# Gated MLP in a decode backward pass: w2 in blocks of 128 rows, and its second half mixed with head 0

## The chip, the core and the metric

The kernel runs on one core of a Trainium2 chip. The metric is device time in microseconds for one launch, taken as the median of repeated runs. Engine names are those of the profile: PE is TensorE's matmul, PEld its weight load, DVE is VectorE, ACT is ScalarE, POOL is GpSimd, SP is SyncE. A letter q after an engine's name means its queue of DMA issues or its sequencer.

## The reference

The kernel computes a forward pass and its vector-Jacobian product for one token. Everything is bf16.

```python
xn  = layernorm(x)                                   # x: 1 x 640
A   = attention(xn @ wq, k_cache, v_cache) @ wo      # 32 heads, 8192 keys, head size 128
B   = (silu(xn @ w1) * (xn @ w3)) @ w2               # gated MLP, 640 -> 1728 -> 640
out = x + A + B
# returned: out, and the gradients for x, k_cache, v_cache, wq, wo, w1, w3, w2
```

The K and V caches (67 MB each) are read once, and gradients of the same size are written. The MLP's three weights have 2.21 MB each; each is read, and a gradient of its size is written.

With the incoming gradient g, the MLP's backward pass needs dh = w2 g, then dgate and dup (1728 values each), and from these dw1 = xn times dgate, dw3 = xn times dup, dw2 = h times g, and a part of the gradient of xn that sums over w1 and w3.

## The kernel before

**Loads and stores.** All loads of weights and caches are issued by SP, in program order, and nearly all stores by POOL, in program order. An issue waits until the tile it fills is free, and everything behind it in the same queue waits too. DVE, SP, POOL and ACT run in the order in which the program was written (`ORDERED`, L58); only PE's order is left to a scheduler.

SP's order at the start is: x, w1 (L142), w3 (L144), w2 in three tiles (L149), wq and wo of the first group of heads, K of head 0, V of heads 0 and 1. `kpool` has three buffers (L68), and w1, w3 and K of head 0 take them. K of head 1 (`load_k(1)`, L544) therefore goes into the buffer of w1 once the store of w1's gradient has landed, and K of head 2 (L545) into that of w3 once its gradient's store has landed: both gradients are computed in place.

**The MLP** is a generator, `mlp_steps` (L440). Its first half runs ahead of `prep_steps(0)` (query and output gradient of the first four heads), its second half after it:

- First half. `gu_ps` (L444 to L449): gate and up as columns, 16 groups of 108 rows of the hidden size; per group five matmuls with a 128 x 108 weight tile of w1 or w3, each streaming one column. Then dh: for each of the three tiles of w2 (6, 5 and 5 groups, on 108 partitions) DVE multiplies by g (L459), PE sums over runs of 64 (L462), DVE finishes the sum (L455). Then a chain of small operations on DVE (L471 to L484) and the diagonal tile `diag` (L486).
- Second half. Eight matmuls spread dgate and dup over all partitions (L496), ACT and DVE copy them to `bc_sb` (L500, L502). Then w2 gives its part of the output (80 matmuls, L509), ACT writes w2's gradient over w2 (16 operations, L511) and POOL stores it in three DMAs (L512). Last, for w1 and then for w3: DVE multiplies the weight by `bc_sb` (three operations, L518), PE sums them into `dx_ps` (54 matmuls, L521), DVE writes the gradient over the weight (L524) and POOL stores it (L528). The tiles `T` that DVE fills for PE have two buffers (`tpool`, L72), which L518 shares with the heads' products.

Since POOL's queue is in order, the store of w1's gradient stands behind all three stores of w2's.

**The heads.** The loop over h (L547) interleaves head h with the start of head h+1. It starts at h = -1, where only the first half of head 0's work is done: `product` S twice (L333 on DVE, L335 on PE), `row_max`, `product` DP twice around `exps`. From h = 0 on, each head has four products for the next head and four `outer` stores of 1 MB each (L342 on DVE, L346 on ACT, L348 on POOL). V of head h+2 and K of head h+3 are loaded as the buffers come free.

Of the kernel before, what the change touches and what calls it, by code (L numbers as in the profile page):

```python
# [16 lines left out]
P = 128  # L17
# [4 lines left out]
def kernel(  # L22
# [38 lines left out]
    R2 = 16  # L61
    FR = F // R2
    ACT_J = 8
    assert H % GW == 0 and GW % GH == 0 and F % R2 == 0 and FR <= P and P % GH == 0
# [29 lines left out]
    w2_v = B_w2.rearrange("(r q) c -> q r c", r=R2)  # L94
    dw2_v = out_8.rearrange("(r q) c -> q r c", r=R2)

    with tc.manual_schedule(engines=ORDERED):
# [43 lines left out]
        w1t = kpool.tile([P, NC, F], BF16, name="w1t", tag="K")  # L141
        nc.sync.dma_start(w1t[:], w1_v)  # L142
        w3t = kpool.tile([P, NC, F], BF16, name="w3t", tag="K")
        nc.sync.dma_start(w3t[:], w3_v)  # L144
        w2_parts = []
        r0 = 0
        for rows in (6, 5, 5):
            w2c = opool.tile([P, rows, D], BF16, name="w2c", tag="o")
            nc.sync.dma_start(w2c[0:FR], w2_v[:, r0:r0 + rows, :])  # L149
            w2_parts.append((r0, rows, w2c))  # L150
            r0 += rows
        assert r0 == R2
# [287 lines left out]
        def mlp_steps():  # L440
# [3 lines left out]
            gu_ps = ps_w.tile([P, 2, R2], F32, name="gu_ps", tag="w")  # L444
            for wi, wt in enumerate((w1t, w3t)):
                for r in range(R2):
                    for ci in range(NC):
                        nc.tensor.matmul(gu_ps[0:FR, wi, r:r + 1], lhsT=wt[:, ci, r * FR:(r + 1) * FR],
                                         rhs=xn_col_bf[:, ci:ci + 1], start=(ci == 0), stop=(ci == NC - 1))  # L449
            dhc = small.tile([P, R2], F32, name="dhc", bufs=1)  # L450
            sums = []

            def dh_reduce():
                r0, rows, dh_ps = sums.pop(0)
                nc.vector.tensor_reduce(dhc[0:FR, r0:r0 + rows], dh_ps[0:FR], AX.X, ALU.add)  # L455

            for k, (r0, rows, w2c) in enumerate(w2_parts):
                T2 = tpool.tile([P, rows, D], BF16, name="T2", tag="T")
                nc.vector.tensor_tensor(T2[0:FR], w2c[0:FR], g_bc_bf[0:FR].unsqueeze(1).to_broadcast([FR, rows, D]), ALU.mult)  # L459
                dh_ps = ps_w.tile([P, rows, DRUN], F32, name="dh_ps", tag="w")  # L460
                for i in range(D // DRUN):
                    nc.tensor.matmul(dh_ps[0:FR], lhsT=ident_bf[0:FR, 0:FR], rhs=T2[0:FR, :, DRUN * i:DRUN * (i + 1)],  # L462
                                     start=(i == 0), stop=(i == D // DRUN - 1))
                sums.append((r0, rows, dh_ps))
                if k:
                    dh_reduce()
            dh_reduce()
            sm_f = small.tile([P, 9, R2], F32, name="sm_f", bufs=1)
            gate, up, th, sig, silu, hcol, t1, dgate, dup = (sm_f[0:FR, i, :] for i in range(9))
            dgu = sm_f[0:FR, 7:9, :]  # L470
            nc.vector.tensor_copy(sm_f[0:FR, 0:2, :], gu_ps[0:FR])  # L471
            nc.scalar.activation(th, gate, ACTF.Tanh, scale=0.5)
            dh = dhc[0:FR]
            nc.vector.tensor_scalar(sig, th, 0.5, 0.5, ALU.mult, ALU.add)
            nc.vector.tensor_tensor(silu, gate, sig, ALU.mult)
            nc.vector.tensor_tensor(dup, dh, silu, ALU.mult)
# [4 lines left out]
            nc.vector.tensor_tensor(dgate, dh, up, ALU.mult)  # L481
            nc.vector.tensor_tensor(dgate, dgate, t1, ALU.mult)
            dgu2 = small.tile([P, 2, R2, 2], BF16, name="dgu2", bufs=1)
            nc.vector.tensor_copy(dgu2[0:FR], dgu.unsqueeze(3).to_broadcast([FR, 2, R2, 2]))  # L484
            diag = opool.tile([P, 2, R2, FR // 2, 2], BF16, name="diag", tag="o")
            nc.vector.tensor_tensor(diag[0:FR],  # L486
                                    ident_bf[0:FR, 0:FR].rearrange("p (a b) -> p a b", b=2).unsqueeze(1).unsqueeze(1)
                                    .to_broadcast([FR, 2, R2, FR // 2, 2]),
                                    dgu2[0:FR].unsqueeze(3).to_broadcast([FR, 2, R2, FR // 2, 2]), ALU.mult)
            bc_sb = opool.tile([P, 2, F], BF16, name="bc_sb", tag="o")  # L490
            yield
            RC = 4
            for wi in range(2):
                for r0 in range(0, R2, RC):
                    bc_ps = ps_w.tile([P, RC, FR], F32, name="bc_ps", tag="w")
                    nc.tensor.matmul(bc_ps[:], lhsT=ones_bf[0:FR, :],  # L496
                                     rhs=diag[0:FR, wi, r0:r0 + RC].rearrange("p r a b -> p r (a b)"), start=True, stop=True)
                    part = bc_sb[:, wi, r0 * FR:(r0 + RC) * FR].rearrange("p (r q) -> p r q", r=RC)
                    if wi == 0 and r0 % (2 * RC) == 0:
                        nc.vector.tensor_copy(part, bc_ps[:])  # L500
                    else:
                        nc.scalar.copy(part, bc_ps[:])  # L502
            nc.vector.tensor_tensor(hcol, silu, up, ALU.mult)
            hcol_bf = small.tile([P, R2], BF16, name="hcol_bf", bufs=1)
            nc.vector.tensor_copy(hcol_bf[0:FR], hcol)
# [36 lines left out]
        for _ in mlp:  # L542
            pass
# [3 lines left out]
        for h in range(-1, H):  # L547
            n = new_head(h + 1) if h + 1 < H else None
            c = hs.pop(h) if h >= 0 else None
            if h >= 0:  # L550
                g, hh = divmod(h, GH)
# [5 lines left out]
            if c:  # L557
                probs(c)
                outer(c, c.do, c.P2, c.Pf, dvc, h, 0)
                if prev:  # L560
                    keep_dq(prev)
# [99 lines left out]
```

## Time and profile before

| | us |
|---|---|
| median of 3 runs (lowest to highest) | 761.67 (760.68 to 762.18) |
| the profiled execution: its own time | 761.41 |
| the profiled execution: span of instructions | 759.4 |
| moved in the span | 303.72 MB, mean 400 GB/s |
| DVE busy | 632.5 (83%) |
| PE busy | 557.3 (73%) |
| ACT busy | 474.4 (62%) |

The profile shows for each engine its busy time, for each of 40 slices of 19 us the busy share in tenths, the granted clock of PE, and what the 16 DMA engines moved. A view by stretches gives the same for any stretch of time: busy time of each engine (with the number of instructions), the granted clock, the share of time that the DMA engines were busy, and GB/s. The timeline lists instructions in order: start, duration, engine, line, operation, what is written from what, and in brackets how long the engine was idle before and what ended that. A view of waits sums idle time by what ended it; the chain is the work that ended last, followed back from the last instruction.

### The profile page before, as it was taken

Reading aid. Unit: us, or ns where it says so; the run is one execution under the profiler, and the core shown is the slowest. Engines: PE = TensorE matmul, PEld = TensorE weight load, DVE = VectorE, ACT = ScalarE, POOL = GpSimd, SP = SyncE. Lnnn points to the kernel's source line nnn. Section 1 sums busy time; section 2 is a strip of 40 time slices with the busy share of each in tenths; the row PEclk is TensorE's granted clock in tenths of the full one; section 3 lists DMA queues with packets and bytes.
Section 4 is the critical chain, followed back from the end, with each engine's and each line's share of the span. In section 5 each row is a group of like instructions: output and inputs, shape, how many; then the busy total and the mean of one; then the engine's idle time right before and its main releaser. Section 6 shows DMA issues by size and latency. Waiting matters only on the chain.

```text
span 759.4 us, 15976 instructions
## 1 busy us (share of the span) xinstructions
PE 557.3 (73%) x6528; PEld 337.3 (44%) x6543; DVE 632.5 (83%) x706; ACT 474.4 (62%) x1421; POOL 87.5 (12%) x166
## 2 busy tenths in 40 slices
PE   6865888878688773877777765788786778777860
PEld 5652445544454442544443433444353445444440
DVE  2577999999799894998788994999887998899970
ACT  2180567777666763787655963778564957677672
POOL 0010011111001120110100120111000111011120
PEclk9987778787886687787896987777795888877665
DMA  8969799999999999999999999999999999999795
GB/s 298 335 258 366 301 428 425 423 422 418 430 427 428 423 416 426 426 423 417 429 428 426 426 377 430 424 427 419 430 425 427 428 418 427 428 427 424 325 363 201
DMA packets 37355, 303.72 MB, mean 400 GB/s; under 512 B 4120, under 2 KB 5874, under 8 KB 12194
## 3 DMA queue, kind: packets, MB, share of 16 engines
q1 hardware_dynamic: 15190, 151.35, 48.5%
q0 software_dynamic: 22080, 151.35, 48.4%
q8 instruction: 51, 0.84, 0.4%
q14 instruction: 22, 0.18, 0.1%
q10 hardware_dynamic: 12, 0.00, 0.0%
HBM read 151.34 MB, written 151.34 MB: 399 GB/s over the span
## 4 chain that ended last, share of the span: by engine, by line
DMA 55%; DVE 31%; PE 6%; issue 4%; ACT 2%; SPq 1%; POOL 0%; POOLq 0%; DVEq 0%; ACTq 0%
DMA out_dram<-ot 39%; DVE T L333 14%; DVE ot L342 11%; DMA out_dram<-wo_g 9%; DMA wo_g<-in_A_wo_dram 4%; DMA w2c<-in_B_w_dram 3%; PE psS L335 2%; ACT ot L346 1%; DVE S_sb L352 1%; DVE DP_sb L386 1%; PE psDP L335 1%; PE dx_ps L521 1%; DVE w3t L524 1%; DVE T L518 1%; SPq L149 0%
## 5 line engine op out<-in xcount | busy, mean ns | idle before, releaser
L335 PE MATMUL psDP<-T,ident_bf 128*128 128x512 bf16 x512 | 187.2, 529 | 65.3 <-DVE T L333 65.3
L335 PEld LDWEIGHTS <-ident_bf 128*128 128x128 bf16 x1024 | 120.2, 120 | 221.8 <-issue 167.0
L346 ACT ACTIVATE ot<-qs_g,Uf 128x128 bf16<-128x128 bf16 x512 | 156.4, 389 | 68.6 <-DMA out_dram<-ot 55.9
L346 ACT ACTIVATE ot<-do_g,Pf 128x128 bf16<-128x128 bf16 x512 | 156.3, 389 | 13.4 <-DMA out_dram<-ot 12.5
L333 DVE TENSOR_TENSOR T<-Kt,qs_g 128x4096 bf16<-128x4096 bf16 x64 | 146.4, 2289 | 2.4 <-PE psDP L335 1.3
L335 PE MATMUL psS<-T,ident_bf 128*128 128x512 bf16 x512 | 141.2, 426 | 9.4 <-DVE T L333 9.4
L333 DVE TENSOR_TENSOR T<-Vt,do_g 128x4096 bf16<-128x4096 bf16 x64 | 146.0, 2281 | 1.4 <-DMA Vt<-in_A_v_cache_dram 1.4
L342 DVE TENSOR_TENSOR ot<-qs_g,U 128x3072 bf16<-128x3072 bf16 x64 | 112.2, 1753 | 40.5 <-DMA out_dram<-ot 40.5
L348 POOL DMA_DIRECT2D out_dram<-ot x128 | 68.2, 533 | 546.3 <-ACT ot L346 192.8
L342 DVE TENSOR_TENSOR ot<-do_g,P 128x3072 bf16<-128x3072 bf16 x64 | 112.3, 1755 | 4.5 <-DMA out_dram<-ot 3.4
L399 PEld LDWEIGHTS <-Kt 128*128 128x128 bf16 x2048 | 57.2, 97 | 12.0 <-issue 9.3
L399 PE MATMUL ob<-U,Kt 128*128 128x1 bf16 x2048 | 57.2, 164 | 2.5 <-issue 1.2
L379 PEld LDWEIGHTS <-Vt 128*128 128x128 bf16 x2048 | 57.1, 97 | 0.0
L379 PE MATMUL ob<-P,Vt 128*128 128x1 bf16 x2048 | 56.9, 163 | 0.0
L365 PEld LDWEIGHTS sm<-rsum,ones_f 128*128 128x128 f32 x64 | 16.4, 282 | 52.7 <-ACT E L364 47.2
L364 ACT ACTIVATE E<-S_sb,negM 128x64 f32<-128x64 f32 x32 | 11.0, 343 | 44.8 <-DVE negM L361 44.7
L245 ACT COPY woT<-ps_t 128x512 bf16<-128x512 bf16 x40 | 22.8, 576 | 25.9 <-PE ps_t L240 25.9
L418 ACT ACTIVATE dq_diag<-ident_bf,odq 128x128 bf16<-128x128 bf16 x32 | 12.8, 399 | 41.2 <-DVE odq L414 41.2
L356 PE MATMUL sm<-ident_f,mrow 128*128 128x128 f32 x64 | 17.6, 361 | 23.8 <-DVE mrow L354 23.0
L373 ACT ACTIVATE Pf<-E,rZ 128x16 f32<-128x16 f32 x32 | 9.8, 307 | 39.2 <-DVE rZ L369 39.2
L352 DVE TENSOR_REDUCE S_sb<-psS 128x64 f32<-128x512 f32 x32 | 21.9, 685 | 11.2 <-PE psS L335 11.2
L262 PE MATMUL ps_d<-woT,G_rep 128*128 128x512 bf16 x33 | 13.4, 405 | 22.6 <-ACT woT L245 22.6
(145 smaller groups left out, 542.4 us busy)
## 6 DMA issues: line engine op xcount, KB each, us to landing
out_dram<-ot POOLq DMA_DIRECT2D x128, 1024.0 KB, 28.4
Kt<-in_A_k_cache_dram SPq DMA_DIRECT2D x32, 2048.0 KB, 17.6
Vt<-in_A_v_cache_dram SPq DMA_DIRECT2D x32, 2048.0 KB, 14.0
wq_g<-in_A_wq_dram SPq DMA_DIRECT2D x4, 1280.0 KB, 24.2
wo_g<-in_A_wo_dram SPq DMA_DIRECT2D x8, 640.0 KB, 9.9
out_dram<-wo_g POOLq DMA_DIRECT2D x8, 640.0 KB, 23.9
out_dram<-wq_g POOLq DMA_DIRECT2D x15, 256.0 KB, 20.4
w1t<-in_B_w_dram SPq DMA_DIRECT2D x1, 2160.0 KB, 8.3
```

Of the source, the lines that this page charges most:

```text
L245: nc.scalar.copy(woT[:], ps_t[:])
L262: nc.tensor.matmul(ps_d[:], lhsT=G_rep[:, ci, :], rhs=woT[:], start=(ci == 0), stop=(ci == NC - 1))
L333: nc.vector.tensor_tensor(T[:], src[:, :, ds_], vec[:, ds_].unsqueeze(1).to_broadcast([P, J, DHH]), ALU.mult)
L335: nc.tensor.matmul(ps[:], lhsT=ident_bf[:], rhs=T[:, :, RUN * i:RUN * (i + 1)], start=(half == 0 and i == 0), stop=(half == 1 and i == DHH ...
L342: nc.vector.tensor_tensor(ot[:, 0:JD], vec.rearrange("p (a b) -> p a b", b=2).unsqueeze(1).to_broadcast([P, JD, DH // 2, 2]), w2[:, j0:j0 ...
L346: nc.scalar.activation(ot[:, j].rearrange("p a b -> p (a b)"), vec, ACTF.Copy, scale=wf[:, half, j - JD:j - JD + 1])
L348: nc.gpsimd.dma_start(dst[h][:, j0:j0 + JH, :], ot[:].rearrange("p j a b -> p j (a b)"))
L352: nc.vector.tensor_reduce(st.S[:], st.ps["S"][:], AX.X, ALU.add)
L356: nc.tensor.matmul(st.sm[:, 8:8 + P], lhsT=mrow[:].to_broadcast([P, P]), rhs=ident_f[:], start=True, stop=True, skip_group_check=True)
L365: nc.tensor.matmul(st.sm[:, 3:4], lhsT=ones_f[:], rhs=rsum[:], start=True, stop=True, skip_group_check=True)
L379: mm = nc.tensor.matmul(st.ob[:, 0:1], lhsT=st.V[:, j, :], rhs=st.P2[:, j, 0:1], start=(j == 0), stop=(j == J - 1), skip_group_check=True)
L399: nc.tensor.matmul(st.ob[:, 1:2], lhsT=st.K[:, j, :], rhs=st.U2[:, j, 0:1], start=(j == 0), stop=(j == J - 1), skip_group_check=True)
```

## The change

w2 is cut into 13 blocks of 128 rows and one of 64, in three tiles of 6, 6 and 2 blocks on all 128 partitions. Its loads are issued first, ahead of w1 and w3; the part of the last tile that the 64-row block leaves empty is set to zero by POOL. dh is computed first, from w2; gate and up follow, as 14 groups with 128 x 128 weight tiles (the last with 128 x 64). The spreading of dgate and dup works in blocks of 128 columns, and `diag` is made in two halves.

The second half is no longer one piece. Ahead of `prep_steps(0)` stand now: the spreading, the gradient of w2's first tile with its store, the work on w1 and the store of w1's gradient. After `prep_steps(0)`: the gradients of w2's second and third tiles, and the multiplications and sums for w3. Then both products S of head 0; then w3's gradient and its store; then `row_max`, the products DP and `exps` of head 0; and last the sum of `dx_ps`. The loop over heads starts at h = 0, and what stood under h = -1 is written ahead of it. POOL's order becomes: w2's first tile, w1's gradient, w2's second tile, the third in two DMAs, w3's gradient.

```diff
-    R2 = 16
-    FR = F // R2
+    NF, REST = divmod(F, P)
+    NB = NF + 1
...
         w1t = kpool.tile([P, NC, F], BF16, name="w1t", tag="K")
+        w3t = kpool.tile([P, NC, F], BF16, name="w3t", tag="K")
+        w2_parts = []
+        for b0 in range(0, NB, 6):
+            nb = min(6, NB - b0)
+            nfull = min(nb, NF - b0)
+            w2c = opool.tile([P, nb, D], BF16, name="w2c", tag="o")
+            if nfull < nb:
+                nc.gpsimd.memset(w2c[:, nfull, :], 0.0)
+            nc.sync.dma_start(w2c[:, 0:nfull, :], w2_v[:, b0:b0 + nfull, :])
+            if nfull < nb:
+                nc.sync.dma_start(w2c[0:REST, nfull, :], B_w2[NF * P:F, :])
+            w2_parts.append((b0, nb, nfull, w2c))
         nc.sync.dma_start(w1t[:], w1_v)
-        w3t = kpool.tile([P, NC, F], BF16, name="w3t", tag="K")
         nc.sync.dma_start(w3t[:], w3_v)
-        for rows in (6, 5, 5):
-            w2c = opool.tile([P, rows, D], BF16, name="w2c", tag="o")
-            nc.sync.dma_start(w2c[0:FR], w2_v[:, r0:r0 + rows, :])
...
+            gu_ps = ps_w.tile([P, 2, NB], F32, name="gu_ps", tag="w")
+            for wi, wt in enumerate((w1t, w3t)):
+                for b, rows in blocks:
+                    for ci in range(NC):
+                        nc.tensor.matmul(gu_ps[0:rows, wi, b:b + 1], lhsT=wt[:, ci, b * P:b * P + rows],
+                                         rhs=xn_col_bf[:, ci:ci + 1], start=(ci == 0), stop=(ci == NC - 1))
...
+            w2_grad(0)
+            dx_part(0, w1t)
+            w_grad(0, w1t, dw1_v)
+            yield
+            w2_grad(1)
+            w2_grad(2)
+            dx_part(1, w3t)
+            yield
+            w_grad(1, w3t, dw3_v)
+            yield
             nc.vector.tensor_reduce(dxn_mlp[:], dx_ps[:], AX.X, ALU.add)
...
         mlp = mlp_steps()
         next(mlp)
         for _ in prep_steps(0):
             pass
-        for _ in mlp:
-            pass
+        next(mlp)
+        first = new_head(0)
+        product(first, "S", 0)
+        product(first, "S", 1)
+        next(mlp)
+        row_max(first)
+        product(first, "DP", 0)
+        exps(first)
+        product(first, "DP", 1)
+        next(mlp, None)
         load_k(1)
         load_k(2)
```

`w2_grad(k)` holds what L507 to L512 did for one tile, `dx_part` what L515 to L523 did for one weight, and `w_grad` what L524 to L528 did.

## The prediction

> **What bounds the kernel now.** I read the page first: which resource is full, and where. Dots are left-out lines.
>
> ```profile
> PE 557.3 (73%) x6528; PEld 337.3 (44%) x6543; DVE 632.5 (83%) x706; ACT 474.4 (62%) x1421; POOL 87.5 (12%) x166
> ...
> DMA  8969799999999999999999999999999999999795
> GB/s 298 335 258 366 301 428 425 423 422 418 430 427 428 423 416 426 426 423 417 429 428 426 426 377 430 424 427 419 430 425 427 428 418 427 428 427 424 325 363 201
> ...
> DMA 55%; DVE 31%; PE 6%; issue 4%; ACT 2%; SPq 1%; POOL 0%; POOLq 0%; DVEq 0%; ACTq 0%
> ```
>
> From slice 6 to slice 36 the DMA engines are full at about 427 GB/s. 303.72 MB at that rate are 711 us, so 48 us of the span are time in which DMA moved less than it could, and the first five slices hold half of them. The change moves hardly a byte more or less. So its worth is the DMA time that it fills or empties before the engines are full for good; the tail stays. The stretches show where that time lies (columns: stretch, length, busy time and count of PE, PEld, DVE, ACT, POOL, granted clock, DMA share, GB/s).
>
> ```profile
> 5.00:10.00 5.00, 1.11 (x8) 1.03 (x9) 2.24 (x8) 2.02 (x3) 0.00 (x0) 1.00 1.01 429
> ...
> 15.00:20.00 5.00, 5.00 (x56) 5.00 (x56) 0.30 (x1) 0.00 (x0) 0.00 (x0) 1.00 0.95 238
> 20.00:25.00 5.00, 5.00 (x51) 4.88 (x51) 1.98 (x2) 0.00 (x0) 0.00 (x0) 1.00 1.11 230
> ...
> 45.00:50.00 5.00, 3.65 (x47) 3.48 (x45) 4.12 (x2) 5.00 (x8) 1.06 (x1) 0.87 0.44 152
> 50.00:55.00 5.00, 1.48 (x10) 1.36 (x10) 5.00 (x3) 3.51 (x5) 2.15 (x3) 0.82 0.65 220
> ...
> 80.00:85.00 5.00, 4.30 (x62) 2.45 (x60) 4.82 (x8) 4.40 (x15) 0.53 (x1) 0.95 0.17 70
> ...
> 120.00:125.00 5.00, 4.71 (x87) 3.31 (x86) 4.97 (x7) 4.75 (x15) 0.53 (x1) 1.00 1.01 424
> ```
>
> There are two holes. From 42 to 56 us the loads are done and few stores exist; at 80 to 85 us K of heads 1 and 2 has arrived and the first head has stored nothing. (At 15 to 25 us DMA is busy but slow: short rows.) Next the timeline, for what ends the holes, and SP's waits.
>
> ```profile
> 9.47 7.54 PEld L448 LDWEIGHTS <-w1t 128*108 128x108 bf16 x80 [3.77 <-DMA w1t<-in_B_w_dram]
> ...
> 41.02 1.85 PEld L509 LDWEIGHTS <-w2c 108*128 108x128 bf16 x65
> ...
> 41.89 11.62 ACT L511 ACTIVATE w2c<-g_bc_bf,sm_f 108x640 bf16<-108x640 bf16 x16
> ...
> 46.94 4.66 DVE L524 TENSOR_TENSOR w1t<-bc_sb,xn 128x8640 bf16<-128x8640 bf16 x1
> ...
> 51.52 3.82 DVE L518 TENSOR_TENSOR T<-w3t,bc_sb 128x3456 bf16<-128x3456 bf16 x2
> ...
> 54.74 0.57 POOL L528 DMA_DIRECT2D out_dram<-w1t  x1
> ...
> 62.65 0.57 POOL L528 DMA_DIRECT2D out_dram<-w3t  x1 [7.33 <-DVE w3t L524]
> ```
>
> ```profile
> SPq L108 <- DMA out_dram<-w1t: 42.4, 1, 42.4
> ...
> SPq L108 <- DMA out_dram<-w3t: 7.2, 1, 7.2
> ```
>
> ```profile
> 78.11 2.29 DVE L333 TENSOR_TENSOR T<-Kt,qs_g 128x4096 bf16<-128x4096 bf16 x1 [1.26 <-PE psDP L335]
> ...
> 83.65 0.53 POOL L348 DMA_DIRECT2D out_dram<-ot  x1 [20.44 <-DVE junk L389]
> ```
>
> w1's gradient is ready at 51.6 (46.94 + 4.66), but its store is issued at 54.74: POOL first waits for ACT's sixteen w2 rows. SP has waited 42.4 us for it with K of head 1 and all later loads behind. DVE is the chain through both holes; at 78.11 it begins head 1's first product, and 5.54 us later comes the first head store. From there DMA stays full. I call 78.11 the loop's start.
>
> **The change part by part.** All against the profiled execution (761.41 us; the median, 761.67, is 0.26 above it).
>
> *Loads.* Before, w1 and w3 go first: 4.42 MB from 2.2 us at 429 GB/s, 10.3 us. Afterwards w2 does: 2.21 MB at the 230 GB/s of 20 to 25 us take 9.6 us, to 11.8. Then w1 to 17.0 and w3 to 22.2. w1 lands at 9.44 now (issued 1.14, 8.3 to landing), 2.1 after its last byte by the rate; w3 at 15.55, 3.0 after. So w1 lands near 19.1 and w3 near 24.7. dh hides in this: three DVE passes (2.16, 2.16, 0.8), PE sums of 2.7 and 2.7 and about 1, all over before 19. POOL's new memset of 128 x 640 stands ahead of the identity that PE needs for dh; the row of a 128 x 128 memset is 0.20 us, so between 0.2 and 1.0 us, done at 2 to 3 us, long before w2's first tile (near 8).
>
> *Gate and up.* Now 80 weight tiles of 108 columns take 7.54 us, 94 ns each. The row of w2c has tiles of 128 columns: 65 in 1.85 us, 28 ns. I take 28 for 65 tiles and 56 (94 scaled to 64 columns) for the five short ones: 2.1 us per weight; by 94 throughout 6.6. So gate and up end at 26.8; at 94 ns, w1 ends at 25.7 and w3 at 32.3. "TensorE: Matmul & The Clock Gate" in the Trainium skill (Weight-path perf modes) says that the fast weight load is on when the weights are 128 and not FP32, and gives it about 2x: 47 ns and 3.3 us, 1.2 us later than I take, which would make the sum 757.8 against the median. The row of this case shows 3.3x, and the row decides.
>
> *Small chain and spreading.* Today from the copy of gu at 32.94 to the end of `dgu2` at 35.22: 2.3 us; a memset and one more copy at 0.17 each: 2.65, to 29.45. Half of `diag` is 1.0 (1.96 x 1792/3456), to 30.5. First matmul and copy start 0.86 later, copies at 0.72 (0.61 x 512/432); the second diagonal and the two h operations end at 34.3. There DVE starts on w1, now 40.42: 6.1 us earlier. `prep_steps`, which stood in between on PE and ACT, is what made way.
>
> *w1.* Products, PE's waits and gradient take 40.42 to 51.6 now, 11.2 us: to 45.5. POOL has only the first w2 tile ahead of it. ACT: bc copies to about 37, six rows at 0.726 (11.62/16) to 41.4; so the store issues at 45.5, not 54.74. It takes 11.2 to land, with K of head 1 behind it: issued near 56.7, not 66.06. Data starts some 3 us later and lasts 4.9 at 427 GB/s, landing near 66.
>
> *prep, on ACT after 41.4:* 0.6 for qs, five copies with PE's turn between (`dx_ps` holds one of three work banks, so no second turn is ahead): about 1.3 each where two overlapped, to 47.3; do_g 1.3, to 49. w2's other eight rows: to 54.7. Their stores issue at 53.3 and 54.7, one DMA more than before at 0.95, over long before w3's at 61.3. Their 1.2 MB go between w1's store and K of head 1, in time that would be empty.
>
> *w3 and head 0.* Products start at 45.5; the last PE matmul of `prep` stands among the first dx matmuls and needs ACT's copy of 47.3: just in time (DVE's first product ends at 47.45). Today PE ends the second block's sums 6.6 after DVE's start, and S needs that buffer: S at 52.1, then 54.35 to 56.6. w3's gradient to 61.25, its store at 61.3 instead of 62.65. PE sums S under it (6.1 us from 54.4). S_sb, mrow 0.95, DP 2.25 to 64.45; the next T waits for PE (3.6): loop start 68.1. negM, DP and the dx sum (0.2, 2.25, 0.65) end before. Lead: 10.0 us.
>
> *The debt.* The store of w3 leads by only 1.4 us, so K of head 2 is issued at 72.2 (61.3 + 10.9 to landing) instead of 73.72. Before, its 2.10 MB had moved by the first head store; now the first head store comes at 68.1 + 5.54 = 73.65, with K's data just starting. 2.10 MB at 427 GB/s are 4.9 us that full DMA must carry later. It is needed at 68.1 + 18.73 (one loop turn, 78.11 to 96.84) = 86.8; sharing half the rate from 74.5 it lands near 86. A small stall there is covered, as DMA is full.
>
> *Sum:* -10.0 + 4.9 = -5.1 us: 756.3 against 761.41, and 756.6 against the median. Bounds: no debt at all gives 751.4; a lead of 4.5 (gate and up at 94 ns, 5.5 late) gives 761.8.
>
> On the loads, "DMA: Bandwidth & Descriptors" in the Trainium skill (Why a DMA increments its semaphore by 16 and not by 1) says that a load on 108 partitions uses 12 of the 16 engines and one on 128 all 16. This trace has a share of 0.95 at 15 to 20 us, which shows at most 0.3 us of idle engines there; by the rule alone the old w2 load would have taken 16/12 of mine, 12.8 us, and the sum would stay as it is, since mine starts from a stretch with a share of 1.11.
>
> **Rivals.**
>
> *A, slower: the mixed PE order stalls w3.* One `prep` matmul inside the dx sums waits for ACT's fifth copy. If that comes late, DVE, w3's store, K of head 2 and the loop all slip. It decides at 5.1 us late (copy ending at 52.4): above that the debt exceeds the lead. ACT's order speaks for it: six w2 rows (4.4 us) now stand ahead of `prep`. Against: I count it done at 47.3. At 8 us late: 764.3.
>
> *B, no change: gate and up stay at 94 ns*, or the copies through one bank eat the lead: lead 4.5, debt 4.9, 761.8. Against: every 128-column row of this profile is near 28 ns.
>
> *C, the DVE chain passes whole.* The chain through the first loop turns is DVE's, so 10 us go to the end: 751.4. Against: DMA at 1.01 and 424 GB/s already at 120 us; no room for the debt.
>
> **How the numbers follow.** Forecast (2 to 8 us gained, 753.5 to 759.7) 0.50; C and better 0.11; B 0.13; A 0.26. A measurement tells 0.2%, 1.5 us, from no change. Faster 0.61, same 0.13, slower 0.26. Predicted 756.6; the range from C's 751.4 to A's 764.3 leaves out under 2 in 10; the forecast's own range is 753.5 to 759.7.
>
> **What would show it.** Weight loads of gate and up at about 28 ns; store of w1 at 45 to 46 us; K of head 1 issued near 57; loop start near 68; a hole shrunk at 42 to 56 and one left near 70, before K of head 2. Wrong if w3's store slips past 66, if gate and up take over 5 us per weight, or if later slices fall under 420 GB/s.

## The result, and the profile after

| | before | after |
|---|---|---|
| median, us (lowest to highest, 4 runs each) | 761.17 (760.37 to 762.18) | 751.29 (749.32 to 751.80) |
| the profiled execution, us | 761.41 | 750.92 |
| its span, us | 759.4 | 749.1 |

The ratio after to before is 0.9865, with a 95% interval from 0.9842 to 0.9887: 9.9 us faster by the medians, 10.5 us by the profiled executions. The forecast was 756.6, with a range from 751.4 to 764.3; the measured median lies just below its lower end. The direction was right and the gain was about twice what was forecast.

From the page of the kernel after, the busy share of the DMA engines and what they moved in 40 slices:

```profile
DMA  9978999999999999999999999999999999999796
GB/s 341 415 281 326 421 427 426 422 424 427 425 433 422 422 419 425 426 423 418 431 426 425 425 380 425 426 428 420 429 429 423 429 415 430 427 424 425 311 367 197
```

The plateau of about 425 GB/s now begins in slice 5 instead of slice 6, and from there on the two rows are alike. The whole gain lies ahead of it. The stretches of the same kernel (length, busy time and count of PE, PEld, DVE, ACT and POOL, granted clock, DMA share, GB/s) show where:

```profile
5.00:10.00 5.00, 0.76 (x3) 0.63 (x4) 4.66 (x11) 1.96 (x3) 0.00 (x0) 1.00 1.14 384
10.00:15.00 5.00, 5.00 (x18) 2.42 (x17) 3.03 (x3) 0.00 (x0) 0.00 (x0) 1.00 0.96 404
15.00:20.00 5.00, 3.00 (x84) 2.69 (x82) 0.86 (x3) 0.00 (x0) 0.00 (x0) 1.00 0.98 411
20.00:25.00 5.00, 2.18 (x70) 2.19 (x71) 1.70 (x12) 0.21 (x1) 0.00 (x0) 0.65 1.08 416
...
45.00:50.00 5.00, 4.58 (x61) 4.17 (x60) 2.86 (x3) 4.47 (x6) 0.00 (x0) 1.00 0.68 287
50.00:55.00 5.00, 3.61 (x16) 1.45 (x15) 5.00 (x3) 3.01 (x5) 1.94 (x3) 1.00 0.56 157
...
65.00:70.00 5.00, 3.79 (x17) 1.45 (x15) 4.82 (x8) 2.99 (x11) 0.00 (x0) 0.92 0.54 183
```

The slow stretch of the loads is gone: no stretch from 5 to 25 us is below 384 GB/s. These stretches mix loads, and the size of the packets tells them apart: a row of w2 is a packet of 1280 bytes, a row of w1 or w3 one of 17,280. From 4 to 8 us only w2 comes in, at 375 GB/s; by 10 us it is w1's turn. The first line below is the view by stretches, the other two are the DMA view of 4 to 8 and of 10 to 15 us:

```profile
4.00:8.00 4.00, 1.13 (x4) 0.96 (x4) 3.04 (x11) 2.94 (x4) 0.00 (x0) 1.00 1.07 375
...
DMA packets 1189, 1.50 MB, mean 375 GB/s; under 512 B 17, under 2 KB 1189, under 8 KB 1189
...
DMA packets 133, 2.02 MB, mean 404 GB/s; under 512 B 16, under 2 KB 16, under 8 KB 16
```

The first hole is shallower and the second, now at 65 to 70 us, is still there. The timeline of the kernel after, at the places that the prediction dated:

```profile
15.93 1.98 PEld L470 LDWEIGHTS <-w1t 128*128 128x128 bf16 x70
...
20.56 2.10 PEld L470 LDWEIGHTS <-w3t 128*128 128x128 bf16 x70 [2.65 <-DMA w3t<-in_B_w_dram]
...
29.55 3.82 DVE L529 TENSOR_TENSOR T<-w1t,bc_sb 128x3456 bf16<-128x3456 bf16 x2
...
42.11 0.55 POOL L541 DMA_DIRECT2D out_dram<-w1t  x1 [4.53 <-DVE w1t L537]
...
51.27 17.49 SPq L108 DMA_DIRECT2D Kt<-in_A_k_cache_dram  x2
...
58.09 0.57 POOL L541 DMA_DIRECT2D out_dram<-w3t  x1 [4.25 <-DVE w3t L537]
...
64.51 2.29 DVE L336 TENSOR_TENSOR T<-Kt,qs_g 128x4096 bf16<-128x4096 bf16 x1 [0.69 <-PE psDP L338]
...
70.06 0.53 POOL L351 DMA_DIRECT2D out_dram<-ot  x1 [11.40 <-DVE junk L392]
```

POOL issues w1's store as soon as DVE's gradient exists (42.11; before 54.74), K of head 1 goes out at 51.27 (before 66.06), the loop starts at 64.51 (before 78.11), and the first head store at 70.06 (before 83.65). That is a lead of 13.6 us. But w3's store leads by 4.6 us only, and K of head 2, the second issue of the merged row, issued at 68.4 (that row ends at 51.27 + 17.49 = 68.76, and an issue takes 0.33), by 5.3 us (before: 73.7).

A lead of 13.6 us and a gain of 10.3 us of span leave 3.3 us to explain. I lay the two kernels' stretches side by side at the first head store. Before:

```profile
0.00:83.65 83.65, 58.35 (x491) 43.20 (x492) 52.13 (x70) 27.23 (x49) 5.23 (x14) 0.88 0.87 309
83.65:123.65 40.00, 33.37 (x438) 20.11 (x440) 39.44 (x42) 25.66 (x86) 4.79 (x9) 0.83 0.98 400
83.65:93.65 10.00, 7.15 (x143) 5.02 (x144) 9.93 (x9) 7.41 (x24) 1.59 (x3) 0.85 0.91 324
93.65:123.65 30.00, 26.22 (x297) 15.10 (x296) 29.51 (x34) 18.26 (x62) 3.20 (x6) 0.82 1.01 425
```

After:

```profile
0.00:70.06 70.06, 45.22 (x462) 29.59 (x462) 51.04 (x73) 26.24 (x47) 5.74 (x15) 0.83 0.87 341
70.06:110.06 40.00, 34.75 (x438) 20.97 (x439) 39.44 (x42) 25.67 (x86) 4.79 (x9) 0.74 0.99 413
70.06:80.06 10.00, 8.08 (x144) 5.42 (x145) 9.93 (x9) 7.41 (x24) 1.60 (x3) 0.80 0.96 377
80.06:110.06 30.00, 26.67 (x296) 15.55 (x294) 29.51 (x34) 18.26 (x62) 3.20 (x6) 0.73 1.01 425
```

Before its first head store, the kernel before had moved 83.65 x 309 = 25.85 MB, the kernel after 70.06 x 341 = 23.89 MB. So the changed kernel starts its heads 13.6 us sooner and owes 1.96 MB, 4.6 us at 427 GB/s. In the next 40 us it moves 0.52 MB (1.2 us) more than the other did, since before it was the DMA that was not full there: 324 GB/s against 377 in the first ten us. 13.6 - 4.6 + 1.2 = 10.2 us, and the spans differ by 10.3. Both kernels run at 425 GB/s afterwards. The same account can be made at a fixed time: 367 GB/s over the first 110 us against 327 are 4.40 MB, 10.3 us.

### The profile page after: what moved, and what is told of

Its sections match the earlier page's. It is cut to its first block, busy times and chain, and to the rows that moved or that the text cites. A ratio compares the mean times of both kernels' runs of the same rounds, so it can differ in the third digit from the quotient of the medians.

```text
span 749.1 us, 15938 instructions
## 1 busy us (share of the span) xinstructions
PE 546.1 (73%) x6513; PEld 323.6 (43%) x6513; DVE 631.8 (84%) x709; ACT 473.3 (63%) x1419; POOL 88.0 (12%) x168
## 4 chain that ended last, share of the span: by engine, by line
DMA 61%; DVE 28%; PE 6%; issue 2%; ACT 1%; SPq 0%; POOL 0%; POOLq 0%; DVEq 0%; ACTq 0%
DMA out_dram<-ot 44%; DVE T L336 12%; DVE ot L345 11%; DMA out_dram<-wo_g 11%; DMA wo_g<-in_A_wo_dram 4%; DMA w3t<-in_B_w_dram 2%; PE psS L338 2%; PE dx_ps L532 1%; DVE S_sb L355 1%; DVE DP_sb L389 1%; DVE w3t L537 1%; PE ps_t L243 1%; PE psDP L338 0%; DVE P L374 0%; ACT woT L248 0%
## 5 line engine op out<-in xcount | busy, mean ns | idle before, releaser
L338 PE MATMUL psDP<-T,ident_bf 128*128 128x512 bf16 x512 | 181.3, 515 | 63.6 <-DVE T L336 63.6
L338 PE MATMUL psS<-T,ident_bf 128*128 128x512 bf16 x512 | 143.3, 430 | 4.5 <-DVE T L336 4.4
L402 PEld LDWEIGHTS <-Kt 128*128 128x128 bf16 x2048 | 57.5, 98 | 13.7 <-issue 11.6
L248 ACT COPY woT<-ps_t 128x512 bf16<-128x512 bf16 x40 | 23.0, 576 | 28.8 <-PE ps_t L243 28.6
L421 ACT ACTIVATE dq_diag<-ident_bf,odq 128x128 bf16<-128x128 bf16 x32 | 12.8, 399 | 40.5 <-DVE odq L417 40.5
L265 PE MATMUL ps_d<-woT,G_rep 128*128 128x512 bf16 x40 | 16.3, 408 | 21.9 <-ACT woT L248 21.7
L243 PE MATMUL ps_t<-ident_bf,wo_g 128*128 128x128 bf16 x160 | 16.9, 233 | 20.2 <-DMA wo_g<-in_A_wo_dram 18.4
## 6 DMA issues: line engine op xcount, KB each, us to landing
Vt<-in_A_v_cache_dram SPq DMA_DIRECT2D x32, 2048.0 KB, 13.9
```

The lines of the kernel that those rows point to most:

```text
L243: nc.tensor.transpose(ps_t[:, hh * DH:(hh + 1) * DH], wo_g[:, hh, ci * P:(ci + 1) * P], ident_bf[:])
L248: nc.scalar.copy(woT[:], ps_t[:])
L265: nc.tensor.matmul(ps_d[:], lhsT=G_rep[:, ci, :], rhs=woT[:], start=(ci == 0), stop=(ci == NC - 1))
L338: nc.tensor.matmul(ps[:], lhsT=ident_bf[:], rhs=T[:, :, RUN * i:RUN * (i + 1)], start=(half == 0 and i == 0), stop=(half == 1 and i == DHH ...
L402: nc.tensor.matmul(st.ob[:, 1:2], lhsT=st.K[:, j, :], rhs=st.U2[:, j, 0:1], start=(j == 0), stop=(j == J - 1), skip_group_check=True)
```

## The experiments

The theories that the runs were to tell apart:

**Theory 1, the bytes.** What counts is how many bytes have moved by the time the DMA engines are full for good. A loop that starts later or earlier without other transfers being ready changes little.

**Theory 2, the chain.** The time follows the start of the loop: each us by which DVE begins the loop sooner is one us of gain, and the missing 3.3 us were lost elsewhere.

The diffs are against the kernel after where nothing else is said. All are timed against the kernel before; its median was between 760.75 and 760.99 us beside the experiments. "By the bytes" is the difference in GB/s over the first 110 us to the 327 of before, times 110 us, over 427 GB/s. It is an account made afterwards from each run's own trace, not a forecast: every kernel moves the same bytes, and from 110 to 700 us all of them run at 423 or 424 GB/s, so that the first 110 us hold the difference.

| run | median us | ratio to before [95%] | loop start | GB/s 0 to 110 | gain by the bytes | gain of the profiled execution |
|---|---|---|---|---|---|---|
| after | 751.29 | 0.9865 [0.9842, 0.9887] | 64.51 | 367 | 10.3 | 10.5 |
| e1_w3_grad_first | 751.61 | 0.9876 [0.9859, 0.9892] | 67.11 | 361 | 8.8 | 8.9 |
| e2_loop_late | 752.15 | 0.9885 [0.9870, 0.9899] | 69.06 | 362 | 9.0 | 9.3 |
| e3_half_weights | 752.54 | 0.9889 [0.9874, 0.9903] | 67.04 | 360 | 8.5 | 8.4 |
| e4_weights_early | 747.99 | 0.9828 [0.9812, 0.9845] | 66.91 | 378 | 13.1 | 12.5 |
| e5_w2_loaded_last | 757.89 | 0.9956 [0.9938, 0.9973] | 70.43 | 344 | 4.4 | 4.3 |
| e6_108_rows_first | 770.06 | 1.0114 [1.0097, 1.0131] | 87.3 | 292 | -9.0 | -8.8 |
| e7_w2_all_ahead | 752.22 | 0.9883 [0.9869, 0.9896] | 69.24 | 359 | 8.2 | 9.2 |
| e8_108_columns | 755.45 | 0.9926 [0.9907, 0.9945] | 68.84 | 350 | 5.9 | 5.6 |
| e9_prep_ahead | 753.35 | 0.9896 [0.9883, 0.9910] | 69.75 | 357 | 7.7 | 7.9 |
| e10_weights_early_w3_first | 748.08 | 0.9829 [0.9812, 0.9846] | 67.53 | 381 | 13.9 | 13.7 |
| e11_k1_before_v1 | 747.22 | 0.9810 [0.9797, 0.9824] | 64.33 | 380 | 13.7 | 13.9 |
| e12_k1_and_w2_ahead | 747.87 | 0.9826 [0.9812, 0.9839] | 68.22 | 377 | 12.9 | 13.9 |

Over thirteen kernels the bytes of the first 110 us give the gain within 1.0 us, from -9 to +14. The loop's start does not: 64.51 goes with 751.3 and 64.33 with 747.2; 66.91 goes with 748.0 and 67.11 with 751.6.

Two cautions. The four runs of the kernel after span 2.5 us, so differences of less than about 1 us between two of these medians are not resolved. And the start of the loop varies by itself: PE starts on w3 between 20.23 and 20.69 us in the kernel after, e2, e8, e10 and e11, and between 21.66 and 21.97 in e1, e3, e4, e7, e9 and e12, though none of these edits changes the loads of w2, w1 and w3. So 1.0 to 1.7 us of a later start in the latter six are not their edit's.

Theory 1 as a forecast was less exact than as an account. Its ranges held for e1, e4 and e7 and were missed by at most 0.4 us for e2, e11 and e12, and by more for e5, e6, e9 and e10.

### e2: the loop late, nothing else

```diff
         next(mlp, None)
+        Tw = tpool.tile([P, J, DH // 2], BF16, name="Tw", tag="T")
+        for _ in range(2):
+            nc.vector.tensor_tensor(Tw[:], first.V[:, :, 0:DH // 2],
+                                    first.do[:, 0:DH // 2].unsqueeze(1).to_broadcast([P, J, DH // 2]), ALU.mult)
         load_k(1)
```

The products are extra work that nothing reads.

> Two DVE products of 2.29 us whose result nobody uses stand ahead of the loop over heads; all else as in the changed kernel. The loop starts 4.5 us later (69.0), K of head 2 is issued at the same 68.8. Theory 1: DMA moves K of head 2 in the time won, so most of the delay costs nothing: 1 to 2 us slower than the changed kernel, 752.3 to 753.3. Theory 2: the whole 4.5 us, 755.8 us.

The timeline of this run:

```profile
64.53 4.62 DVE L578 TENSOR_TENSOR Tw<-Vt,do_g 128x4096 bf16<-128x4096 bf16 x2 [0.69 <-PE psDP L338]
69.06 2.28 DVE L336 TENSOR_TENSOR T<-Kt,qs_g 128x4096 bf16<-128x4096 bf16 x1
```

The loop starts 4.55 us later, and the median is 752.15, 0.9 us more than that of the kernel after. Theory 2 needed 4.5 us, and falls (theory 1's range of 752.3 to 753.3 began 0.15 us too high): while DVE was late, K of heads 1 and 2 went on arriving, so the debt shrank by most of what the lead lost.

### e4: 1.97 MB of loads moved into the hole

wo of group 1 and wq of the next groups are loaded behind V of head 1, not in the loop's first turn.

```diff
         load_v(1)
+        load_wo(1)
+        load_wq(1)
...
-                if (g + 1) % HB == 0:
+                if (g + 1) % HB == 0 and g + 1 > HB:
                     load_wq((g + 1) // HB)
-                load_wo(g + 1)
+                if g + 1 > 1:
+                    load_wo(g + 1)
```

> The loads of wo for the second group of heads and of the second wq (1.97 MB, buffers free from the start) are issued behind V of head 1 instead of inside the loop. They fall into the stretch from 40 to 58 us in which DMA is busy for two thirds. Loop start as in the changed kernel, 64.5, or up to 1 later. Theory 1: 1.97 MB at 427 GB/s are 4.6 us, less what w1's store loses beside them: 746.7 to 749 us. Theory 2: nothing, 751.3 us.

747.99, 3.3 us better than the kernel after. The loop started 2.4 us later, waiting for K of head 1. That load was issued 2.7 us later (54.01 against 51.27): w1's store went out 1.3 us later, and it took 10.5 us to land instead of 9.0, with the added loads beside it. From the timeline:

```profile
66.91 2.29 DVE L338 TENSOR_TENSOR T<-Kt,qs_g 128x4096 bf16<-128x4096 bf16 x1 [3.10 <-DMA Kt<-in_A_k_cache_dram]
```

A kernel whose loop starts later by a real wait for DMA is faster, since more bytes have moved by then. That is theory 1 from the other side.

### e11 and e12: the same bytes, two starts

e11 is e4 with K of head 1 loaded at the start in the place of V of head 1, and V of head 1 in w1's buffer. e12 is e11 with all of w2's gradient ahead of the work on w1.

```diff
-            Kt = kpool.tile([P, J, DH], BF16, name="Kt", tag="K")
+            pool, tag = (vpool, "V") if h == 1 else (kpool, "K")
+            Kt = pool.tile([P, J, DH], BF16, name="Kt", tag=tag)
...
-            Vt = vpool.tile([P, J, DH], BF16, name="Vt", tag="V")
+            pool, tag = (kpool, "K") if h == 1 else (vpool, "V")
+            Vt = pool.tile([P, J, DH], BF16, name="Vt", tag=tag)
...
-        load_v(1)
+        load_k(1)
+        load_wo(1)
+        load_wq(1)
...
         next(mlp, None)
-        load_k(1)
+        load_v(1)
```

> wo of the second group and the second wq loaded early, and K of head 1 loaded at the start in the buffer of V of head 1, which goes behind w1's store instead. The loop no longer waits for w1's store. Theory 1 (unfilled DMA time): the loop starts at 64.5 again instead of 66.9 as with the early loads alone, 2 us better than those: 745 to 747 us. Theory 2 (the loop's start alone): as the changed kernel, 751.3 us.

```diff
# e12: as e11, and
             w2_grad(0)
+            w2_grad(1)
+            w2_grad(2)
             dx_part(0, w1t)
...
-            w2_grad(1)
-            w2_grad(2)
             dx_part(1, w3t)
```

> The kernel with the early loads and K of head 1 first, and w2's gradient all ahead of the work on w1. The stores of w2's second and third tiles move from 52 to about 40 us, where DMA still has loads, and leave the stretch at 50 to 55 us emptier; w3's store has less beside it and lands sooner. Theory 1: the two cancel within 1 us of the kernel without the second edit, 744.5 to 747.5 us. Theory 2: 751 to 753 us.

The loop's start in e11:

```profile
64.33 2.29 DVE L340 TENSOR_TENSOR T<-Kt,qs_g 128x4096 bf16<-128x4096 bf16 x1 [0.69 <-PE psDP L342]
```

and in e12:

```profile
68.22 2.29 DVE L340 TENSOR_TENSOR T<-Kt,qs_g 128x4096 bf16<-128x4096 bf16 x1 [0.69 <-PE psDP L342]
```

The starts are 3.9 us apart (1.6 of them because w3 lands later in e12); the profiled executions are 747.53 and 747.56, the medians 747.22 and 747.87. e11 is the best kernel of the study: 0.9810 [0.9797, 0.9824] of the kernel before and 4.1 us below the changed kernel's median. In e11 the loop waits for nothing from DMA, and the wait of 3.10 us of e4 is gone, but that is worth 0.8 us at most, which the medians hardly resolve. Both medians lie just above the ranges of theory 1 (by 0.2 and 0.4 us) and far below those of theory 2.

### e5 and e6: is it w2's place or its shape that loads fast?

In e5 w2 has blocks of 128 rows and is loaded last, as before. In e6 the kernel before keeps its blocks of 108 rows and loads them first.

```diff
# e5
-            nc.sync.dma_start(w2c[:, 0:nfull, :], w2_v[:, b0:b0 + nfull, :])
...
         nc.sync.dma_start(w3t[:], w3_v)
+        for b0, nb, nfull, w2c in w2_parts:
+            nc.sync.dma_start(w2c[:, 0:nfull, :], w2_v[:, b0:b0 + nfull, :])
...
# e6, against the kernel before
-        nc.sync.dma_start(w1t[:], w1_v)
-        nc.sync.dma_start(w3t[:], w3_v)
...
         assert r0 == R2
+        nc.sync.dma_start(w1t[:], w1_v)
+        nc.sync.dma_start(w3t[:], w3_v)
```

> The changed kernel with its 128-row blocks, but loads in the old order: w1, w3, w2. If the 128-row form is what makes w2's load fast, the stretch after 13 us, in which w2 is loaded, shows over 350 GB/s, dh ends near 24 and the loop starts 1 to 2 us later: 752.3 to 753.3 us. If it was fast for being first, that stretch stays near 235 GB/s, dh ends near 28 and the time is 755 to 757 us.

> The kernel before with its 108-row groups, but w2 loaded ahead of w1 and w3. If the 108-row form is slow, the first 12 us show about 170 to 240 GB/s; if w2 was slow for its place behind w1 and w3, they show 400. The gate and up columns keep their 94 ns and the chain of small operations starts near 31 us instead of 32.9, so by both theories on the end 759 to 761 us.

Stretches in which nearly all packets are w2's. Of e5, with 128 rows at the old place:

```profile
14.00:19.00 5.00, 0.00 (x0) 0.00 (x0) 1.54 (x1) 0.00 (x0) 0.00 (x0) 1.00 1.07 366
```

of the kernel before, with 108 rows at the old place:

```profile
14.00:17.00 3.00, 3.00 (x35) 3.00 (x35) 0.00 (x0) 0.00 (x0) 0.00 (x0) 1.00 0.80 204
```

and of e6, with 108 rows at the new place, first while w2 is alone and then with w1 beside it:

```profile
4.00:6.00 2.00, 1.18 (x4) 1.00 (x4) 1.29 (x5) 1.62 (x3) 0.00 (x0) 1.00 0.80 298
7.00:13.00 6.00, 0.00 (x0) 0.00 (x0) 4.55 (x3) 0.51 (x1) 0.00 (x0) 1.00 1.11 246
```

The shape decides. On 128 partitions w2 alone comes in at 366 GB/s at its old place and at 375 at its new one; on 108 partitions at 204 and 298. Counted by its packets, the whole load takes about 7 us on 128 partitions at either place, and about 15 (old place) and 11 us (new place) on 108. The place is worth something too, on 108 partitions, but less.

On 108 partitions the DMA engines show a share of 0.80 while w2 is alone, three quarters of the 1.07 on 128, so some of them are idle there. In e6, w1's packets begin at 6.5 us, while w2 is still loading. From then on the share is 1.11, but the rate falls to 246 GB/s: w2's packets take about 100 ns each instead of 55, w1's about 1.0 us instead of 0.65. Why the two slow each other was not tried.

Both times missed their expectations by a wide margin, 757.89 and 770.06, by an order on PE that I had not looked up. In e5 PE's program has dh ahead of gate and up, so w1, long landed, waits for w2: gate and up of w1 begin at 25.30, of w3 at 27.24, and the loop starts at 70.43. In e6 it is the reverse: PE stands at gate and up of w1 until w1, now last, is there.

```profile
19.30 7.62 PE L448 MATMUL gu_ps<-xn_col_bf,w1t 128*108 128x1 bf16 x80 [13.39 <-DMA w1t<-in_B_w_dram]
```

dh's sums stand behind it, and the loop starts only at 87.3. So moving w2's load ahead costs 9 us if PE's order stays as it was; the change moved both. The account by the bytes holds for both (4.4 and 4.3; -9.0 and -8.8 us).

### e3 and e8: the width of the weight tiles of gate and up

e3 cuts each 128 x 128 tile into two of 64 columns. e8 keeps the aligned starts but loads only the first 108 of each 128 columns; the other 20 columns of gate and up are left out and taken as zero.

```diff
# e3
-                    for ci in range(NC):
-                        nc.tensor.matmul(gu_ps[0:rows, wi, b:b + 1], lhsT=wt[:, ci, b * P:b * P + rows],
+                    for r0 in range(0, rows, 64):
+                        for ci in range(NC):
+                            nc.tensor.matmul(gu_ps[r0:r0 + 64, wi, b:b + 1],
+                                             lhsT=wt[:, ci, b * P + r0:b * P + r0 + 64],
...
# e8
-                        nc.tensor.matmul(gu_ps[0:rows, wi, b:b + 1], lhsT=wt[:, ci, b * P:b * P + rows],
+                        nc.tensor.matmul(gu_ps[0:min(rows, 108), wi, b:b + 1],
+                                         lhsT=wt[:, ci, b * P:b * P + min(rows, 108)],
```

> Gate and up with 64-column weight tiles, 135 per weight instead of 70, all else as in the changed kernel. If weights under 128 columns load slowly (56 ns, scaled from 94 at 108 columns), gate and up of w3 take 7.6 us instead of 2.1 and everything behind them, stores and loop alike, shifts by 5.5: 756.8 us by both theories. If they load as fast as 128 columns (28 ns each), it shifts by 1.8: 753.1 us.

> The changed kernel with gate and up from the first 108 columns of each block's weight tile, at the tile's aligned start; the other 20 columns of each full block are left out (gate and up are zero there). If a width of 108 is what makes a weight load slow, the 70 matmuls of w3 take 6.6 us instead of 2.2 and the time is 755.7 us; if it was where the old tiles began (steps of 216 bytes), they take 2.2 and the time is 751.3 us.

PE's timeline in e3:

```profile
15.49 2.38 PE L471 MATMUL gu_ps<-xn_col_bf,w1t 128*64 128x1 bf16 x135
...
21.66 3.89 PE L471 MATMUL gu_ps<-xn_col_bf,w3t 128*64 128x1 bf16 x135 [3.79 <-DMA w3t<-in_B_w_dram]
```

and in e8:

```profile
16.33 4.43 PE L470 MATMUL gu_ps<-xn_col_bf,w1t 128*108 128x1 bf16 x70
20.69 6.58 PE L470 MATMUL gu_ps<-xn_col_bf,w3t 128*108 128x1 bf16 x70
```

Tiles of 64 columns take 17.6 ns each for w1 and 28.8 for w3, and the time is 752.54, 1.25 us more. Tiles of 108 columns cost 4.2 us of the whole (755.45), as I had expected if the width is what makes them slow. Here, unlike in e2, w3's 4.4 us pass almost whole: all stores and the loads behind them shift with the loop (w1's store to 46.63, w3's to 62.41, the loop to 68.84).

But it is not the width alone; the granted clock matters. Stretches of e8, for the matmuls into `gu_ps` only (columns: length, PE busy and count, DVE busy and count, granted clock, DMA share, GB/s). The count includes tiles already under way at the start of a stretch, so I take two stretches with the same start and divide the added time by the added tiles:

```profile
16.40:17.40 1.00, 1.00 (x22) 0.00 (x0) 1.00 0.90 380
16.40:18.40 2.00, 2.00 (x42) 0.00 (x0) 1.00 1.04 441
...
21.00:22.00 1.00, 1.00 (x13) 0.00 (x0) 0.50 1.02 371
21.00:26.00 5.00, 5.00 (x56) 0.00 (x0) 0.50 1.10 433
```

and of the kernel after:

```profile
16.00:17.00 1.00, 1.00 (x41) 0.00 (x0) 1.00 0.90 380
16.00:17.50 1.50, 1.50 (x61) 0.00 (x0) 1.00 0.95 403
...
21.50:21.80 0.30, 0.30 (x17) 0.00 (x0) 0.50 1.03 375
21.50:22.10 0.60, 0.60 (x29) 0.00 (x0) 0.50 1.02 375
```

At a granted clock of 1.00 a 108-column tile takes 50 ns (20 more in 1 us); at 0.50 it takes 93 (43 more in 4 us). A 128-column tile takes 25 ns at 1.00 (20 more in 0.5 us) and 25 to 27 at 0.50 (12 more in 0.3 us; 26 or 27 from one start to the next): it hardly feels the clock. e8 pays because its w3 part falls into the low clock. The 64-column tiles of e3 feel it too (17.6 ns where the clock was 1.00, 28.8 at 0.50).

The kernel before took 94 ns per 108-column tile, e8's pace at 0.50, where the view shows a clock of 1.00. e6 tells why: it runs the same tiles twice, w1's from 19.30 and w3's from 33.14 us.

```profile
20.00:21.00 1.00, 1.00 (x13) 0.00 (x0) 1.00 0.87 358
20.00:26.00 6.00, 6.00 (x67) 0.00 (x0) 1.00 0.99 395
33.20:34.20 1.00, 1.00 (x22) 0.00 (x0) 1.00 0.97 410
33.20:34.70 1.50, 1.50 (x32) 0.00 (x0) 1.00 0.98 415
35.00:36.00 1.00, 1.00 (x13) 0.00 (x0) 0.50 0.92 393
35.00:39.00 4.00, 4.00 (x45) 0.00 (x0) 0.50 0.99 422
```

They take 93 ns (54 in 5 us), then 50, then 94. The trace's clock records begin only at 31.32 us in e6, at 29.26 in the kernel before and at 14.64 in the kernel after; ahead of the first record the view shows 1.00 even where PE does nothing. So the first 1.00 is no measurement, and the pace says that the clock was 0.50 there. In each of the three kernels the first record, of 1.00, comes 4.5 to 4.8 us after dh's wide matmuls begin (26.79, 24.42 and 9.82 us); in the kernel before, 15 us of one-column matmuls back to back had not brought it about. The old gate and up were slow for two reasons: tiles of 108 columns, and the low clock that these tiles feel.

### e1, e7 and e9: single pieces of the order

```diff
# e1: w3's gradient ahead of head 0's products S
         next(mlp)
+        next(mlp)
         first = new_head(0)
...
         product(first, "S", 1)
-        next(mlp)
         row_max(first)
# e7: all of w2's gradient and its stores ahead of w1's
             w2_grad(0)
+            w2_grad(1)
+            w2_grad(2)
             dx_part(0, w1t)
...
-            w2_grad(1)
-            w2_grad(2)
             dx_part(1, w3t)
# e9: prep_steps(0) ahead of the spreading, as before
             bc_sb = opool.tile([P, 2, F], BF16, name="bc_sb", tag="o")
+            yield
...
             w_grad(0, w1t, dw1_v)
-            yield
```

> Theory 1 (DMA time left empty before the engines are full sets the time): the loop over heads starts about 3 us later than in the changed kernel (67.6 instead of 64.5, since nothing lies over PE's last sums for S), but w3's gradient is stored at 53.5 instead of 58.1 and K of head 2 is issued near 64 instead of 68.8, so the 1.4 MB that the changed kernel still owes after the first head are moved earlier. The two cancel: 750.3 to 752.3 us. Theory 2 (the DVE chain to the loop's start passes to the end in full): 3 us slower, 754.4 us.

> The changed kernel with all three parts of w2's gradient ahead of the work on w1, as the kernel before had them: w1's store goes behind w2's again, and ACT writes fourteen rows instead of six ahead of the head projections. ACT was idle for 4.4 us there (36.3 to 40.7), so 5.8 us more of rows delay the projections by 1.5 us, w1's store by about 1.5 us, the loop by 0 to 1.5 us: 751.3 to 753 us by both theories. If instead PE's last projection stalls the sums for w3 as the slower rival of the prediction has it: 755 us or more.

> The changed kernel with the projections of the first four heads ahead of the spreading of dgate and dup, as in the kernel before. They wait for wq and wo (loaded near 27 us) and take 5.6 us on ACT and PE as before; DVE starts on w1 near 34 instead of 29.6, and everything behind it shifts by 4 to 5 us: 755 to 756.5 us by both theories.

**e1**: 751.61, as expected, but not for the reason that I had given. From its timeline:

```profile
52.41 17.62 SPq L108 DMA_DIRECT2D Kt<-in_A_k_cache_dram  x2
...
54.57 0.57 POOL L541 DMA_DIRECT2D out_dram<-w3t  x1
```

w3's store goes out 3.5 us sooner, but K of head 2 is issued at 69.7 (the row ends at 52.41 + 17.62 = 70.03), 1.3 us later than in the kernel after. The store took 15.0 us to land instead of 10.2. It was issued 0.5 us behind w2's last store and just behind K of head 1; in e7 and e9, where w2's stores are issued by 49.5 us, it lands in 6.9. In these runs it lands the later, the closer it stands behind them; which of them holds it up was not tried. Storing w3's gradient ahead of head 0's products costs or saves less than the medians resolve (0.3 us).

**e7**: 752.22, 0.9 us slower, though the loop starts 4.7 us later. Here the mechanism of rival A happens:

```profile
50.75 1.06 DVE L529 TENSOR_TENSOR T<-w3t,bc_sb 128x1728 bf16<-128x1728 bf16 x1 [3.90 <-PE dx_ps L532]
...
53.46 4.49 DVE L336 TENSOR_TENSOR T<-Kt,qs_g 128x4096 bf16<-128x4096 bf16 x2 [1.66 <-PE dx_ps L532]
```

DVE waits 5.6 us for PE's sums into `dx_ps`, where it waits 2.1 in the kernel after (1.66 + 0.48). These 3.4 us and the later landing of w3 in this run (1.2) make the loop's 4.7. About 1 us of that reaches the end. K of head 2 is issued only 1.4 us later, since w3's store, free of w2's, lands in 6.9 us.

**e9**: 753.35, 2.1 us slower, where I had expected about twice that. The loop starts 5.2 us later (69.75), as expected, but 1.3 us of that is w3 landing later in this run, and by the later start more bytes have moved, as in e2 (24.9 MB at the first head store, 75.30 us, against 23.89). Putting `prep` behind w1 is thus worth some 2 us of the ten, at this accuracy.

### e10: e4 and e1 together

```diff
# e4's edit, and
         next(mlp)
+        next(mlp)
         first = new_head(0)
...
-        next(mlp)
         row_max(first)
```

> wo of the second group and the second wq loaded early, and w3's gradient stored ahead of head 0's products: both edits tried alone before. In the first alone the loop already waited for K of head 1 until 66.9, about when it starts in the second, so the earlier store of w3's gradient costs nothing here. Theory 1 (unfilled DMA time): K of head 2 moves ahead of the first head store, 1.4 MB or 3.3 us on top of the first edit's 748.0: 744 to 746 us. Theory 2 (DVE chain): 748 to 749 us.

748.08, no better than e4, and above what I expected. w3's store goes out at 53.81 and lands 15.6 us later, so K of head 2 is issued at 69.5 (the row ends at 53.66 + 16.16 = 69.82). This is e1's effect again: a store issued close behind others does not land as much sooner. The time lies in theory 2's range (748 to 749), so this run alone would not speak against that theory; e2 and e11 do.

## Why the prediction was right in direction and short by half

**What failed first: the step "Loads".** It took "2.21 MB at the 230 GB/s of 20 to 25 us" for the new w2 load, 9.6 us: a rate read from the old form, 108 partitions, at the old place, and in a stretch that wq's load shares. Measured on 128 partitions, w2 comes in at 375 GB/s, which makes 5.9 us, and e5 and e6 show that the form makes most of it. With 3.7 us less, w3 would have been forecast near 21.0 instead of 24.7; PE starts on it at 20.56. (The step also has a slip: 22.2 and its own 3.0 us to landing make 25.2, not 24.7.) Nearly all of the 4.1 us reaches the loop: DVE starts on w1 at 29.55 (forecast 34.3), w1's store goes out at 42.11 (45.5), w3's at 58.09 (61.3), the loop starts at 64.51 (68.1). This term made the lead 13.6 us instead of 10.0.

On this "DMA: Bandwidth & Descriptors" in the Trainium skill (Why a DMA increments its semaphore by 16 and not by 1) has a rule that I cited in the prediction, and that I applied the wrong way round: 108 partitions use 12 of the 16 engines. My 9.6 us came from the old form, so by the rule I should have given the new one 12/16 of them, an estimate of 7.2 us, and not the old one 12.8.

The traces agree with the rule where w2 is alone: the share of the DMA engines is 0.80 on 108 partitions (e6, 4 to 6 us; the kernel before, 14 to 17 us) against 1.07 on 128, a ratio of 0.75, and the rates of e6 and of the kernel after are 298 and 375, a ratio of 0.79. My reading "at most 0.3 us of idle engines" took the stretch from 15 to 20 us, in which wq's packets had begun. The rule is not all of it: the whole load takes about 11 us against 7, because it slows further once another load runs beside it (246 GB/s at a share of 1.11). A share near one did not mean that the load could go no faster. Nor were short rows as such the reason, as the prediction had it: rows of 1280 bytes come in at 366 to 375 GB/s on 128 partitions.

**What failed second: "From there DMA stays full", on which the last clause of "The debt" rests.** The debt itself was right: 4.9 us forecast, 4.6 us (1.96 MB) measured at the first head store. But that clause, by which I closed the account of the kernel before, is wrong: it moved 324 GB/s in the ten us after its first head store. The changed kernel moved 377 there, so 1.2 us of the debt came back. Net 3.4 us instead of 4.9. The stretch of 85 to 95 us of the kernel before (363 GB/s) would have told me.

**The sum.** 3.6 us more lead and 1.5 us less debt make 5.1 us of the 5.2 by which the gain (10.3 against 5.1) was short. Both errors have the same sign.

**What held.** Gate and up took 1.98 and 2.10 us per weight (forecast 2.1), so rival B did not come; e8 prices it at 4.2 us, the forecast between B and the likeliest case having been 5.2. `prep` on ACT ended at 47.4 (forecast 49 at the latest), w2's later stores went out at 51.86 and 53.30 (53.3 and 54.7). A hole before K of head 2 remained, at 65 to 70. And the reason that I held against rival C stands: the chain does not pass whole. e2 puts 4.55 us into DVE's chain and pays 0.9. Rival C named 751.4 (751.7 from the median, which is 0.26 us above the profiled execution), and 751.29 was measured; that is luck: two wrong terms add up to C's number, and C's mechanism did not happen.

**Rival A** was priced wrongly. I let every us of a late w3 count in full ("It decides at 5.1 us late"). In e7 the rival's wait makes DVE 3.4 us later at this place, the loop and w3's store are 4.7 us late in all, and the time pays 0.9 us, because a late loop also lets the loads catch up. I had applied the account by bytes to the gain and not to the rival's loss. e7 is not the rival alone, though: it also moves w2's stores out of the way of w3's, so that K of head 2 loses only 1.4 us.

On the weight tiles, "TensorE: Matmul & The Clock Gate" in the Trainium skill (Weight-path perf modes) gives the fast load to 128 weights and about 2x. At a clock of 1.00 the runs show 50 ns at 108 columns against 25 at 128, 2.0x, which agrees. The 3.3x of the prediction compared 94 ns at the low clock with 28 ns; that 28 could be carried over all the same, because the 128-column tiles hardly feel the clock. By the pace of the 108-column tiles, tiles of 64 columns would take 30 and 56 ns; e3's took 17.6 and 28.8.

## What to carry to other kernels

When the DMA engines are full for most of the time, count the bytes that have moved by the moment they become full, for both kernels, and divide the difference by the full rate. Read from their own traces, that one number gives thirteen results within 1.0 us, while kernels whose loops start 0.2 us apart differ by 4 us. It must be applied to losses as well as to gains. Read the rate of a moved load from a load of the new shape, not from its old one, and only from a stretch in which it is alone. What helps next is then found the same way: e11 puts loads that nothing holds back into the hole and gains 4.1 us more.

## What the runs showed of the hardware that was not expected

- A load of w2 alone in the queues ran at 298 GB/s with a DMA share of 0.80 on 108 partitions (e6, 4 to 6 us) and at 375 GB/s with 1.07 on 128 (the kernel after, 4 to 8 us). With w1's packets beside it, e6 moved 246 GB/s in all at a share of 1.11 (7 to 13 us).
- A weight tile of 128 columns with one streamed column took 25 ns at a granted clock of 1.00 and 25 to 27 at 0.50; one of 108 columns took 50 and 93 to 94 ns.
- Ahead of the trace's first clock record (29.26 us in the kernel before) the view shows 1.00, while the tiles run at the pace of 0.50 (94 ns).
- The same store of w3's gradient (2.21 MB) took 10.2 us to land in the kernel after, 15.0 and 15.6 us in e1 and e10, where it was issued 0.5 us behind w2's last store, and 6.9 us in e7 and e9, where w2's stores had gone out more than 13 us before.
